# Windowed and global attention with a fused MLP: query columns in token order, with the global queries' inner scores apart

## The chip, the cores and the metric

The kernel runs on one core of one Trainium2 chip. The metric is the device time of one execution in microseconds (us). "Before" is the kernel as it stood, "after" is the same kernel with the change below.

## What is computed

Attention with 8 batches and 8 heads of width 64. Each head has 512 local tokens and 32 global tokens. Global queries see all 544 keys. Local queries see the 32 global keys and the local keys at most 32 positions away. The 4352 output tokens (544 a batch, global ones first), with the heads put side by side to 512 columns, then go through a two-layer network with a sigmoid-weighted activation. Cut to what matters:

```
k_all = concat([k_g, k_l]);  v_all = concat([v_g, v_l])       # per batch and head
out_g = softmax(scale * q_g @ k_all.T) @ v_all                # 32 x 64
s_ll  = where(|i - j| <= 32, scale * q_l @ k_l.T, -1e9)       # 512 x 512
s_lg  = scale * q_l @ k_g.T                                   # 512 x 32
out_l = softmax(concat([s_lg, s_ll])) @ concat([v_g, v_l])    # 512 x 64
x = concat([out_g, out_l]) as [8 * 544, 512]
h = x @ w_in                                                  # 512 -> 2048
out = (h * sigmoid(1.702 * h)) @ w_out                        # 2048 -> 512
```

Inputs and output are float32. The matmuls take bfloat16 operands and accumulate in float32.

## The kernel before

The order of all work is written out by hand (`manual_schedule`), and each engine runs its instructions in that order. A batch's eight heads are two **quads** of four heads (class `Quad`, with head `j` on the 32 partitions `32j` to `32j+31`; two of the 64 head columns lie in one 4-byte element). For each quad:

- `T` is `Tk` and `Tq`: VectorE transposes 32x32 blocks of the loaded keys and queries (tiles `rk`, `rq`) into `kT` and the query tile `qt` (four of them, used in turn). A loaded row holds 16 tokens, so a transposed block holds, for one `t` of 0 to 15, the tokens `16r+t` of all `r` of 0 to 31. `Tk` writes with a step, so that `kT` is in token order (L271). `Tq` writes its blocks one after the other, so that `qt` is ordered by `t`, then `r` (L275).
- `qt` has 24 such rows `t`: 16 of local queries and 4 at each end that `ext` (L285) fills with copies of the 32 global queries, cut into rows as wide as a window. A window is a range of `r` for each chunk `c` of 128 keys: `WIN = ((0, 10), (6, 12), (14, 12), (22, 10))`, that is 160 or 192 queries.
- `S(rnd)` (L314) computes the scores of two key chunks, `c = 2*rnd` and `2*rnd+1`, for the four heads. For each chunk and each half `e` of the head columns it issues four matmuls, one per head, each on its own 32 rows of the array and into its own PSUM bank. The moving operand is `q[p, lo:hi, r0:r0+nr, e]`: 20 or 19 rows `t` of 10 or 12 queries, 200 or 228 columns. Global and local queries of a chunk thus go in one matmul.
- `gk` (L333) multiplies global keys with queries: `K` for the local queries (512 columns, tile `kb`), `gg` for the global ones (32 columns).
- `X` exponentiates the scores on ScalarE into the tile `E` (L347), `XK` does it for `kb` (L383, with a DMA that copies the result to other partitions), `M` multiplies by the window mask on VectorE (L354), `eg` picks the blocks for the global queries.
- `U(unit)` (L426) adds up the softmax sums (unit 0) and the two halves of the output (units 1, 2) from `E` and `v`, four heads side by side on 32 array columns each; `ekU` (L400) adds the global keys' part. `Gm` (L444) does the global queries' output, four heads with 66 columns.
- `R` and `XL` divide by the sums into `xL`, `G` does so for the global queries into `xG`.

Then the network: `h_mm` (L495) makes 128 of the 2048 columns at a time for a batch's 512 local tokens, `h_act` (ScalarE tanh, VectorE multiply) makes `gT`, and `o_mm` (L520) makes tiles of 128 tokens by 512. `o_out` scales a tile on ScalarE into `ob` and sends it out (L542). Since the tokens of `xL` and `gT` are ordered by `t`, then `r`, a tile of 128 tokens is four groups of 32 rows that lie 16 rows apart in the output, and goes out by four DMAs from the SP queue. The global tokens of all batches are a ninth, narrower batch at the end.

`phase_o(i)` interleaves the output matmuls of batch `i` with the attention of batch `i+1`, two rounds `S` and one `UG` (`ekU`, `U`, `Gm`) per quad; the 16 `h_step` of a batch follow. The first two batches have an order of their own: quad 0 is loaded and transposed in halves, its first round is issued in two parts (`part=0` and `1`, after the first and the second half of `Tq`), and quads 0 and 1 add the mask to the scores by matmuls with an identity (`B`, L297) instead of `M`. Quad 2's `T`, `ext` and first `S` come after the `h_step` of batch 0. The transposition `Tq` of quad 4 and that of its global keys (`transpose_g`, tile `kgT`, L205) stand in the middle of quad 2's output work.

Of the kernel before, what the change touches and what calls it, by code (L numbers as in the profile page):

```python
# [20 lines left out]
def kernel(  # L21
# [24 lines left out]
    HD = D // 2  # L46
# [4 lines left out]
    RW = 428  # L51
# [118 lines left out]
    for i in range(4):  # L170
        qt = consts.tile([128, 24, 32], F32, name="q%d" % i)
        nc.vector.memset(qt[:, 0:4, :], 0.0)
        nc.vector.memset(qt[:, 20:24, :], 0.0)
        qtiles.append(qt)

    WIN = ((0, 10), (6, 12), (14, 12), (22, 10))
# [5 lines left out]
    bias = consts.tile([128, 16, 12], BF16)  # L182
    bandt = band.rearrange("p (r t) -> p t r", t=16)
    nc.vector.tensor_sub(ident, step[:, 65:193], step[:, 64:192])
    nc.vector.tensor_sub(band, step[:, 65:257], step[:, 0:192])
    nc.vector.tensor_scalar(bias, bandt, -1.0, 262144.0, op0=ALU.add, op1=ALU.mult)

    def near(t, c):
        lo = 0 if c else 2
        return t[:, :, lo : lo + WIN[c][1]]  # L190

    def make_mask(c):
        nr = WIN[c][1]
        at = (0, 160, 0, 192)[c]
        nc.scalar.activation(mask[:, c // 2, at : at + 16 * nr].rearrange("p (t r) -> p t r", t=16),
                             near(bandt, c), AF.Copy)

    qgT = consts.tile([128, NQ, 40], F32)
    nc.vector.memset(qgT[:, :, 32:], 0.0)
    kgT = consts.tile([128, NQ, 32], F32)  # L200
    def transpose_g(lo, hi, names="qk"):
        for name, dst, s in (("q", qgT, rqg), ("k", kgT, rkg)):
            if name not in names:
                continue
            nc.vector.transpose(dst[:, lo:hi, :32], s[:, lo:hi].bitcast(F32))  # L205
# [43 lines left out]
    class Quad:  # L249
        def __init__(self, Q):  # L250
            self.Q = Q
            self.b, self.u = divmod(Q, 2)
            if self.u == 0:
                xL[self.b] = att.tile([128, NKC, Sl], BF16, name="xL", bufs=2)
            self.x = xL[self.b]
            self.v = vtiles[self.b % 2][:, self.u]
            self.qt = qtiles[Q % 4]
            self.q = self.qt.bitcast(BF16).rearrange("p t (r e) -> p t r e", e=2)
            self.qg = qgT[:, Q, :32].bitcast(BF16).rearrange("p (s e) -> p s e", e=2)
            self.kg = kgT[:, Q].bitcast(BF16).rearrange("p (s e) -> p s e", e=2)  # L260
            self.E = [None, None]
            self.bk = {}
            self.st = {}
            self.pt = None
            self.gr = 1
# [8 lines left out]
        def Tq(self, lo=0, hi=16):  # L274
            nc.vector.transpose(self.qt[:, 4 + lo : 4 + hi, :].rearrange("p t r -> p (t r)"),  # L275
                                loaded[self.b][1][:, self.u].bitcast(F32)[:, 32 * lo : 32 * hi])
# [5 lines left out]
        def ext(self, cs=(0, 1, 2, 3)):  # L282
            for c in cs:
                (r0, nr), t0, n = WIN[c], (0, 20, 1, 20)[c], (4, 3, 3, 4)[c]
                nc.vector.tensor_copy(  # L285
                    self.qt[:, t0 : t0 + n, r0 : r0 + nr],
                    qgT[:, self.Q, : n * nr].rearrange("p (t r) -> p t r", t=n))


        def B(self, rnd, split=False, js=range(4)):  # L290
            if 0 in js:
                self.bk[rnd] = [pbank("s") for _ in range(4)] if split else self.spt(rnd)
            ps = self.bk[rnd] if split else [bank(self.bk[rnd], j) for j in range(4)]
            for c in (2 * rnd, 2 * rnd + 1):
                w = (40, 200, 36, 228)[c]
                for j in js:
                    nc.tensor.matmul(ps[j][:, w : w + 16 * WIN[c][1]], lhsT=ident, rhs=near(bias, c),  # L297
                                     start=(c == 2 * rnd), stop=False, skip_group_check=True)

        def S(self, rnd, split=False, added=False, part=None):  # L300
            if not added:
                self.bk[rnd] = self.spt(rnd)
            ps = self.bk[rnd] if split else [bank(self.bk[rnd], j) for j in range(4)]
            for c in (2 * rnd, 2 * rnd + 1):
                off = (0, 200, 0, 228)[c]
                r0, nr = WIN[c]
                t0, t1 = ((0, 20), (4, 23), (1, 20), (4, 24))[c]
                lo, hi = ((t0, t1) if part is None else (12, t1) if part else (t0, 12))
                off += (lo - t0) * nr
                n = (hi - lo) * nr  # L310
                for e in range(2):
                    for j in range(4):
                        p = slice(32 * j, 32 * j + 32)
                        nc.tensor.matmul(  # L314
                            ps[j][:, off : off + n],
                            lhsT=self.k[p, 128 * c : 128 * c + 128, e],
                            rhs=self.q[p, lo:hi, r0 : r0 + nr, e],
                            start=(e == 0 and not added), stop=(e == 1), skip_group_check=True,
                        )
            if not part:  # L320
                self.E[rnd] = att.tile([128, 4, RW + 32], BF16, name="e%d" % rnd)
            if split:
                self.gk(ps[2][:, RW : RW + 32], self.qg)
            self.ps = self.bk[rnd]


        def gk(self, out_, rhs, e=None):
            for ee in (0, 1) if e is None else (e,):
                for j in range(4):
# [4 lines left out]
                                     rhs=rv[:, :, ee] if len(rv.shape) == 3 else rv[:, :, :, ee],  # L334
# [16 lines left out]
        def M(self, rnd):  # L351
            at = 36 if rnd else 40
            e = self.E[rnd][:, :, at : at + LW]
            nc.vector.tensor_mul(e, e, mask[:, rnd : rnd + 1, :].to_broadcast([128, 4, LW]))  # L354

        def K(self, e=None):
            if e != 1:
                self.kb = pbank("kb")
            self.gk(self.kb, self.q[:, 4:20], e)
# [57 lines left out]
        def U(self, unit):  # L417
            ov = self.st[unit]
            h = unit - 1
            for c in range(4):  # L420
                r0, nr = WIN[c]
                at = (40, 200, 36, 228)[c]
                for j in range(4):
# [3 lines left out]
                        ov[32 * j : 32 * j + 32, :].rearrange("p (t r) -> p t r", t=16)[:, :, r0 : r0 + nr],  # L427
                        lhsT=lv, rhs=self.E[c // 2][:, j, at : at + 16 * nr],
# [3 lines left out]
        def Gm(self, og=None):  # L432
            if og is None:
                og = pbank("og")
            for c in range(5):
                for j in range(4):
                    if c < 4:
                        at = (0, 392, 0, 388)[c]
                        lv = self.E[c // 2][:, j, at : at + 32]
# [85 lines left out]
    def o_out(i, tci, op):  # L525
        ob = moe.tile([128, d_model], F32, name="ob", bufs=6)
        last = i == B and tci == B // 4 - 1
        for lo, hi in ((0, 320), (320, 512)) if last else ((0, 512),):
# [5 lines left out]
            nc.scalar.activation(ob[:, lo:hi], op[:, lo:hi], AF.Copy, scale=0.5)  # L534
            for j in range(4):
                eng = nc.scalar if last and j % 2 else nc.sync
                if i < B:
                    rows = out[i * S + Sg : (i + 1) * S, :].rearrange("(r t) m -> t r m", t=16)[4 * tci + j]
                else:
                    r = (4 * tci + j) * S  # L540
                    rows = out[r : r + Sg, :]
                eng.dma_start(out=rows[:, lo:hi], in_=ob[32 * j : 32 * j + 32, lo:hi])  # L542
# [22 lines left out]
    a.ext((0, 1))  # L565
# [5 lines left out]
    a.ext((2, 3))  # L571
# [257 lines left out]
```

## Time and profile before

| what | value |
|---|---|
| time, median of 3 runs | 307.43 us (307.39 to 307.59) |
| profiled execution, first to last instruction | 305.3 us, its own time is not given apart from this span |
| PE, DVE, ACT, POOL busy | 298.7, 211.2, 169.3, 55.7 us |
| granted PE clock | 1.00 throughout |
| score matmuls (L314) | 528, 21.2 us busy |
| DMA issues of output tiles from SP | 136, most of 64 KB, median 1.7 us to landing |

PE is the matmul side of TensorE and PEld its weight loads, DVE is VectorE, ACT is ScalarE, POOL is GpSimd, SP the queue that issues DMAs. Busy time is the union of an engine's instructions, so matmuls that overlap count once. A shape such as `32*128 32x228` is a tile of 32 array rows by 128 columns, with 228 moving columns.

### The profile page before, as it was taken

The page shows a single profiled execution, that of the slowest core. Times are in us where ns is not written, and L with a number is a line of the kernel's source. Part 1 is how long each engine was busy: PE and PEld are TensorE (multiplying, and loading weights), DVE is VectorE, ACT ScalarE, POOL GpSimd, SP SyncE. Part 2 cuts the span into 40 slices and gives each one's busy share as a digit, 9 for nine tenths or more (in the row PEclk, how much of TensorE's full clock was granted, in tenths as well). Part 3 has the DMA queues.
Part 4 walks back from the last instruction along what each step waited for, and adds up shares of the span by engine and source line. Part 5 has one row for each costly group of instructions (what it writes and reads, how often), then busy time and mean ns, then how long its engine had stood idle before and what let it go on. Part 6 is the DMA issues. An engine that isn't in the chain of part 4 may idle for free.

```text
span 305.3 us, 7862 instructions
## 1 busy us (share of the span) xinstructions
PE 298.7 (98%) x3265; PEld 148.5 (49%) x3265; DVE 211.2 (69%) x445; ACT 169.3 (55%) x282; POOL 55.7 (18%) x89
## 2 busy tenths in 40 slices
PE   7999999999999999999999999999999999999995
PEld 6454445445454455445454455445454454446653
DVE  6678858978868876777767876787677855573320
ACT  4738484585556655575457654665456661673421
POOL 8732755530050002300050002100000000000000
PEclk9999999999999999999999999999999999999999
DMA  7999999999399023941299024901130021101122
GB/s 191 178 206 207 197 180 230 211 170 131 82 112 191 10 56 84 151 97 37 54 122 170 4 56 89 101 0 48 44 86 2 2 66 48 46 0 36 36 63 75
DMA packets 56436, 29.52 MB, mean 97 GB/s; under 512 B 43088, under 2 KB 46288, under 8 KB 56400
## 3 DMA queue, kind: packets, MB, share of 16 engines
q0 software_dynamic: 46000, 16.98, 49.9%
q1 hardware_dynamic: 9920, 11.39, 14.3%
q10 hardware_dynamic: 480, 0.66, 0.7%
q8 instruction: 25, 0.41, 0.6%
q14 instruction: 11, 0.09, 0.1%
HBM read 35.13 MB, written 8.91 MB: 144 GB/s over the span
## 4 chain that ended last, share of the span: by engine, by line
PE 80%; DMA 15%; DVE 2%; POOL 1%; issue 1%; ACT 0%; ACTq 0%; DVEq 0%; POOLq 0%
PE op L520 34%; PE hp L495 33%; DMA rk<-in_k_l_dram 10%; PE s L314 5%; PE ov L426 4%; DMA rq<-in_q_l_dram 3%; DMA w_in_sb<-in_moe_w_in_dram 2%; PE ov L400 2%; DVE xL L459 1%; PE op L532 1%; PE s L444 1%; PE s L333 1%; ACTq L542 0%; ACT ob L534 0%; DVE e L354 0%
## 5 line engine op out<-in xcount | busy, mean ns | idle before, releaser
L520 PE MATMUL op<-w_out_sb,gT 128*128 128x512 bf16 x528 | 122.0, 380 | 0.0
L503 DVE SCALAR_TENSOR_TENSOR gT<-th,hp 128x512 bf16<-128x512 f32 (+1 forms) x140 | 91.2, 657 | 41.8 <-ACT th L502 40.7
L495 PE MATMUL hp<-xL,w_in_sb 128*128 128x512 bf16 x496 | 108.9, 379 | 0.3 <-DVE xL L459 0.2
L502 ACT ACTIVATE th<-hp 128x512 f32<-128x512 f32 (+1 forms) x140 | 79.9, 573 | 43.4 <-PE hp L495 39.9
L495 PEld LDWEIGHTS <-w_in_sb 128*128 128x128 bf16 x576 | 56.2, 98 | 64.7 <-issue 0.9
L520 PEld LDWEIGHTS <-gT 128*128 128x128 bf16 x528 | 49.2, 98 | 56.2 <-issue 3.5
L347 ACT ACTIVATE e<-s 128x856 bf16<-128x856 f32 x62 | 51.6, 884 | 12.1 <-PE s L444 7.0
L534 ACT ACTIVATE ob<-op 128x512 f32<-128x512 f32 (+2 forms) x35 | 20.5, 585 | 59.0 <-PE op L520 56.5
L89 POOL DMA_DIRECT2D v<-in_v_l_dram x24 | 18.7, 782 | 111.2 <-PE s L444 105.8
L450 DVE STREAM_TRANSPOSE sT<-ov 128x512 f32<-128x512 f32 x15 | 10.8, 717 | 26.9 <-PE ov L426 26.9
L354 DVE TENSOR_TENSOR e<-e,mask 128x1408 bf16<-128x1408 bf16 x28 | 24.4, 872 | 5.7 <-ACT e L347 5.7
L314 PE MATMUL s<-q,kT 32*128 32x228 bf16 (+5 forms) x528 | 21.2, 280 | 1.0 <-DVE q L275 1.0
L459 DVE TENSOR_TENSOR xL<-ov,rs 128x512 bf16<-128x512 f32 x30 | 19.3, 686 | 1.4
L314 PEld LDWEIGHTS <-kT 32*128 32x128 bf16 x528 | 10.9, 95 | 14.8 <-issue 6.6
L271 DVE STREAM_TRANSPOSE kT<-rk 128x512 f32<-128x512 f32 (+1 forms) x17 | 16.9, 994 | 1.0 <-DMA rk<-in_k_l_dram 1.0
L383 ACT ACTIVATE ek<-kb 128x512 bf16<-128x512 f32 x16 | 9.7, 608 | 9.2 <-PE kb L333 7.0
L426 PE MATMUL ov<-e,v 128*32 128x160 bf16 (+1 forms) x480 | 12.2, 239 | 0.0
L454 DVE STREAM_TRANSPOSE rs<-rT 128x512 f32<-128x512 f32 x16 | 11.4, 711 | 0.6
L275 DVE STREAM_TRANSPOSE q<-rq 128x512 f32<-128x512 f32 (+1 forms) x17 | 10.9, 641 | 1.0 <-ACT rq L558 1.0
L426 PEld LDWEIGHTS <-v 128*32 128x32 bf16 x512 | 10.0, 97 | 0.9 <-issue 0.9
L333 PE MATMUL kb<-q,kgT 32*32 32x512 bf16 x128 | 10.4, 387 | 0.0
L495 PE MATMUL hp<-xG,w_in_sb 128*128 128x256 bf16 x64 | 9.6, 273 | 0.0
(82 smaller groups left out, 170.6 us busy)
## 6 DMA issues: line engine op xcount, KB each, us to landing
out_dram<-ob SPq DMA_DIRECT2D x132, 64.0 KB, 1.7
v<-in_v_l_dram POOLq DMA_DIRECT2D x32, 128.0 KB, 6.0
rk<-in_k_l_dram POOLq DMA_DIRECT2D x6, 512.0 KB, 10.8
rq<-in_q_l_dram POOLq DMA_DIRECT2D x5, 512.0 KB, 8.6
w_out_sb<-in_moe_w_out_dram POOLq DMA_DIRECT2D x4, 512.0 KB, 10.8
rq<-in_q_l_dram POOLq DMA_DIRECT2D x5, 256.0 KB, 8.9
ek<-ek SPq DMA_DIRECT2D x13, 96.0 KB, 2.9
w_in_sb<-in_moe_w_in_dram POOLq DMA_DIRECT2D x4, 256.0 KB, 6.4
```

What stands on the lines that cost most here:

```text
L89: nc.gpsimd.dma_start(out=vtiles[b % 2][p, s, :, :, :D], in_=vf[b, g][:, hs])
L271: nc.vector.transpose(self.kT.rearrange("p (r t) -> p t r", t=16)[:, lo:hi], loaded[self.b][0][:, self.u].bitcast(F32)[:, 32 * lo : 32 * hi])
L314: nc.tensor.matmul(ps[j][:, off : off + n], lhsT=self.k[p, 128 * c : 128 * c + 128, e], rhs=self.q[p, lo:hi, r0 : r0 + nr, e], start=(e == ...
L347: nc.scalar.activation(e[:, 2 * i : 2 * i + 2, :RW], self.ps[i][:, :, :RW], AF.Exp, scale=scale)
L354: nc.vector.tensor_mul(e, e, mask[:, rnd : rnd + 1, :].to_broadcast([128, 4, LW]))
L426: nc.tensor.matmul(ov[32 * j : 32 * j + 32, :].rearrange("p (t r) -> p t r", t=16)[:, :, r0 : r0 + nr], lhsT=lv, rhs=self.E[c // 2][:, j, ...
L459: nc.vector.tensor_mul(self.x[:, 2 * self.u + h, :], self.st[1 + h], self.st["rs"])
L495: nc.tensor.matmul(hp[:, : width(i)], lhsT=w_in_c[:, fc // 8, kc, fc % 8 // 2, :, fc % 2], rhs=(xL[i] if i < B else xG)[:, kc, :], start=( ...
L502: nc.scalar.activation(th[:, :n], hp[:, :n], AF.Tanh, scale=0.851)
L503: nc.vector.scalar_tensor_tensor(gTs[i][:, fc, :n], in0=th[:, :n], scalar=1.0, in1=hp[:, :n], op0=ALU.add, op1=ALU.mult)
L520: nc.tensor.matmul(op, lhsT=gTs[i][:, fc, tci * 128 : tci * 128 + 128], rhs=w_out_sb[:, fc, :], start=(first and fc == 4 * f4), stop=(fc = ...
L534: nc.scalar.activation(ob[:, lo:hi], op[:, lo:hi], AF.Copy, scale=0.5)
```

## The change

The query tile holds the queries in token order: 32 global queries, the 512 local ones, and the 32 global ones again. `Tq` writes with a step as `Tk` does. `ext` becomes one copy that fills both ends. A window is a range of tokens, so that the columns of scores, of `E` and of the mask are contiguous token ranges, and PSUM columns of `U` too. For the outer chunks (0 and 3) the global queries adjoin the window, and one matmul of 192 columns covers both. For the inner chunks (1 and 2) they don't, so that there are two matmuls, of 192 and of 32 columns. Both use the same weights, which are loaded for each. In the split first round the local queries of each part are 8 of every 16 columns. `E` is 416 columns wide for a head instead of 428. Output tiles are 128 adjoining rows and go out by one DMA; those of the global tokens are unchanged. The memsets of the query tiles and of `qgT`'s padding go.

```diff
-    RW = 428
+    RW = 416
...
-        qt = consts.tile([128, 24, 32], F32, name="q%d" % i)
-        nc.vector.memset(qt[:, 0:4, :], 0.0)
-        nc.vector.memset(qt[:, 20:24, :], 0.0)
-        qtiles.append(qt)
-
-    WIN = ((0, 10), (6, 12), (14, 12), (22, 10))
+        qtiles.append(consts.tile([128, Sl + 2 * Sg], F32, name="q%d" % i))
+
+    WIN = ((0, 160), (96, 192), (224, 192), (352, 160))
+    AT = (32, 192, 32, 224)
+    GAT = (0, 384, 0, 384)
...
-    bias = consts.tile([128, 16, 12], BF16)
-    bandt = band.rearrange("p (r t) -> p t r", t=16)
+    bias = consts.tile([128, 192], BF16)
...
-    qgT = consts.tile([128, NQ, 40], F32)
-    nc.vector.memset(qgT[:, :, 32:], 0.0)
+    qgT = consts.tile([128, NQ, 32], F32)
...
         def Tq(self, lo=0, hi=16):
-            nc.vector.transpose(self.qt[:, 4 + lo : 4 + hi, :].rearrange("p t r -> p (t r)"),
+            nc.vector.transpose(self.qt[:, Sg : Sg + Sl].rearrange("p (r t) -> p t r", t=16)[:, lo:hi],
                                 loaded[self.b][1][:, self.u].bitcast(F32)[:, 32 * lo : 32 * hi])
...
-        def ext(self, cs=(0, 1, 2, 3)):
-            for c in cs:
-                (r0, nr), t0, n = WIN[c], (0, 20, 1, 20)[c], (4, 3, 3, 4)[c]
-                nc.vector.tensor_copy(
-                    self.qt[:, t0 : t0 + n, r0 : r0 + nr],
-                    qgT[:, self.Q, : n * nr].rearrange("p (t r) -> p t r", t=n))
+        def ext(self):
+            nc.vector.tensor_copy(
+                self.qt.rearrange("p (n w) -> p n w", w=Sg)[:, ::17],
+                qgT[:, self.Q : self.Q + 1].to_broadcast([128, 2, Sg]))
...
         def S(self, rnd, split=False, added=False, part=None):
...
-                off = (0, 200, 0, 228)[c]
-                r0, nr = WIN[c]
-                t0, t1 = ((0, 20), (4, 23), (1, 20), (4, 24))[c]
-                lo, hi = ((t0, t1) if part is None else (12, t1) if part else (t0, 12))
-                off += (lo - t0) * nr
-                n = (hi - lo) * nr
+                q0, w = WIN[c]
+                at = AT[c]
+                if part is None:
+                    runs = {0: ((0, 0, 192),), 1: ((at, Sg + q0, w), (GAT[c], 0, Sg)),
+                            2: ((at, Sg + q0, w), (GAT[c], 0, Sg)), 3: ((at, Sg + q0, 192),)}[c]
+                else:
+                    runs = ((at, Sg + q0, w),) if part else ((at, Sg + q0, w), (GAT[c], 0, Sg))
                 for e in range(2):
-                    for j in range(4):
-                        p = slice(32 * j, 32 * j + 32)
-                        nc.tensor.matmul(
-                            ps[j][:, off : off + n],
-                            lhsT=self.k[p, 128 * c : 128 * c + 128, e],
-                            rhs=self.q[p, lo:hi, r0 : r0 + nr, e],
-                            start=(e == 0 and not added), stop=(e == 1), skip_group_check=True,
-                        )
+                    for k, (o0, i0, n) in enumerate(runs):
+                        for j in range(4):
+                            p = slice(32 * j, 32 * j + 32)
+                            o, r = ps[j][:, o0 : o0 + n], self.q[p, i0 : i0 + n, e]
+                            if part is not None and k == 0:
+                                h = slice(8 * part, 8 * part + 8)
+                                o = o.rearrange("p (r t) -> p r t", t=16)[:, :, h]
+                                r = r.rearrange("p (r t) -> p r t", t=16)[:, :, h]
+                            nc.tensor.matmul(
+                                o, lhsT=self.k[p, 128 * c : 128 * c + 128, e], rhs=r,
+                                start=(e == 0 and k == 0 and not added), stop=(e == 1), skip_group_check=True,
+                            )
...
         def M(self, rnd):
-            at = 36 if rnd else 40
-            e = self.E[rnd][:, :, at : at + LW]
+            e = self.E[rnd][:, :, Sg : Sg + LW]
...
         def U(self, unit):
...
                     nc.tensor.matmul(
-                        ov[32 * j : 32 * j + 32, :].rearrange("p (t r) -> p t r", t=16)[:, :, r0 : r0 + nr],
-                        lhsT=lv, rhs=self.E[c // 2][:, j, at : at + 16 * nr],
+                        ov[32 * j : 32 * j + 32, q0 : q0 + w], lhsT=lv, rhs=self.E[c // 2][:, j, at : at + w],
...
     def o_out(i, tci, op):
...
+            if i < B:
+                r = i * S + Sg + 128 * tci
+                nc.sync.dma_start(out=out[r : r + 128, :], in_=ob)
+                continue
             for j in range(4):
                 eng = nc.scalar if last and j % 2 else nc.sync
-                if i < B:
-                    rows = out[i * S + Sg : (i + 1) * S, :].rearrange("(r t) m -> t r m", t=16)[4 * tci + j]
-                else:
-                    r = (4 * tci + j) * S
-                    rows = out[r : r + Sg, :]
-                eng.dma_start(out=rows[:, lo:hi], in_=ob[32 * j : 32 * j + 32, lo:hi])
+                r = (4 * tci + j) * S
+                eng.dma_start(out=out[r : r + Sg, lo:hi], in_=ob[32 * j : 32 * j + 32, lo:hi])
...
-    a.ext((0, 1))
+    a.ext()
...
     a.Tq(8, 16)
-    a.ext((2, 3))
```

More of the change, by code (lines that the diff above doesn't have):

```diff
@@ L45 @@
     NQ = B * 2
-    HD = D // 2
     NKC = d_model // 128
@@ L181 @@
     band = consts.tile([128, 192], BF16)
-    bias = consts.tile([128, 16, 12], BF16)
-    bandt = band.rearrange("p (r t) -> p t r", t=16)
+    bias = consts.tile([128, 192], BF16)
     nc.vector.tensor_sub(ident, step[:, 65:193], step[:, 64:192])
     nc.vector.tensor_sub(band, step[:, 65:257], step[:, 0:192])
-    nc.vector.tensor_scalar(bias, bandt, -1.0, 262144.0, op0=ALU.add, op1=ALU.mult)
+    nc.vector.tensor_scalar(bias, band, -1.0, 262144.0, op0=ALU.add, op1=ALU.mult)
     def near(t, c):
-        lo = 0 if c else 2
-        return t[:, :, lo : lo + WIN[c][1]]
+        lo = 0 if c else 32
+        return t[:, lo : lo + WIN[c][1]]
     def make_mask(c):
[L193 to L196, printed above, removed]
-    qgT = consts.tile([128, NQ, 40], F32)
-    nc.vector.memset(qgT[:, :, 32:], 0.0)
+        at = AT[c] - 32
+        nc.scalar.activation(mask[:, c // 2, at : at + WIN[c][1]], near(band, c), AF.Copy)
+    qgT = consts.tile([128, NQ, 32], F32)
     kgT = consts.tile([128, NQ, 32], F32)
@@ L204, in transpose_g @@
                 continue
-            nc.vector.transpose(dst[:, lo:hi, :32], s[:, lo:hi].bitcast(F32))
+            nc.vector.transpose(dst[:, lo:hi, :], s[:, lo:hi].bitcast(F32))
     def load_v2(b):
@@ L257, in __init__ @@
             self.qt = qtiles[Q % 4]
-            self.q = self.qt.bitcast(BF16).rearrange("p t (r e) -> p t r e", e=2)
-            self.qg = qgT[:, Q, :32].bitcast(BF16).rearrange("p (s e) -> p s e", e=2)
+            self.q = self.qt.bitcast(BF16).rearrange("p (m e) -> p m e", e=2)
+            self.qg = qgT[:, Q].bitcast(BF16).rearrange("p (s e) -> p s e", e=2)
             self.kg = kgT[:, Q].bitcast(BF16).rearrange("p (s e) -> p s e", e=2)
@@ L294, in B @@
             for c in (2 * rnd, 2 * rnd + 1):
-                w = (40, 200, 36, 228)[c]
+                w = AT[c]
                 for j in js:
-                    nc.tensor.matmul(ps[j][:, w : w + 16 * WIN[c][1]], lhsT=ident, rhs=near(bias, c),
+                    nc.tensor.matmul(ps[j][:, w : w + WIN[c][1]], lhsT=ident, rhs=near(bias, c),
                                      start=(c == 2 * rnd), stop=False, skip_group_check=True)
@@ L333, in gk @@
                     nc.tensor.matmul(out_[r : r + 32], lhsT=self.kg[p, :, ee],
-                                     rhs=rv[:, :, ee] if len(rv.shape) == 3 else rv[:, :, :, ee],
+                                     rhs=rv[:, :, ee],
                                      start=(ee == 0), stop=(ee == 1), skip_group_check=True)
@@ L358, in K @@
                 self.kb = pbank("kb")
-            self.gk(self.kb, self.q[:, 4:20], e)
+            self.gk(self.kb, self.q[:, Sg : Sg + Sl], e)
         def eg(self):
@@ L420, in U @@
             for c in range(4):
-                r0, nr = WIN[c]
-                at = (40, 200, 36, 228)[c]
+                q0, w = WIN[c]
+                at = AT[c]
                 for j in range(4):
@@ L437, in Gm @@
                     if c < 4:
-                        at = (0, 392, 0, 388)[c]
-                        lv = self.E[c // 2][:, j, at : at + 32]
+                        lv = self.E[c // 2][:, j, GAT[c] : GAT[c] + Sg]
                         rv = self.v[:, j, c, :]
```

## The prediction

> **What bounds the kernel now.** I read the page's busy shares first, then the table of stages, then the chain of waits in one steady stretch, and last the start times of single matmuls.
>
> ```profile
> span 305.3 us, 7862 instructions
> ...
> PE 298.7 (98%) x3265; PEld 148.5 (49%) x3265; DVE 211.2 (69%) x445; ACT 169.3 (55%) x282; POOL 55.7 (18%) x89
> ...
> PEclk9999999999999999999999999999999999999999
> ```
>
> PE is busy for 98% of the span at a full granted clock. No other engine passes 69%. A share that high can hide pipelined waiting, so I look at stages:
>
> ```profile
> 57.00:103.44 46.44, 46.33 (x465) 21.77 (x467) 36.94 (x78) 29.03 (x48) 9.80 (x13) 1.00 1.12 134
> 103.44:137.50 34.06, 34.06 (x389) 16.33 (x392) 25.51 (x53) 19.94 (x32) 4.51 (x6) 1.00 0.58 87
> 137.50:171.56 34.06, 34.06 (x389) 16.33 (x392) 25.50 (x53) 19.95 (x32) 4.50 (x6) 1.00 0.58 86
> ```
>
> The columns are the stage, its length, then PE, PEld, DVE, ACT and POOL busy. One batch takes 34.06 us, again and again, and PE fills it. The chain of waits inside one batch names only PE lines:
>
> ```profile
> 137.50 0.60 PE s L314 x16
> 138.10 3.56 PE op L520 x16
> 141.66 0.59 PE s L314 x16
> ...
> 142.88 1.03 PE ov L426 x47
> ```
>
> So from about 57 us on a nanosecond saved on PE is a nanosecond off the end, and DVE, ACT, SP and the transfers have room. Before that, three places hang on DVE (below).
>
> A **round** is one call of `S`: a quad (four heads) against two key chunks, 16 matmuls in the chain above. They run as four sets of four, one matmul per row group of 32 rows, started within about 10 ns of each other. From the start times of single matmuls in the timeline, a set of 200 columns is followed 114.9 ns later by the next (24 cases), one of 228 columns 133.8 ns later (30 cases). The `U` sets (L426) take 70.9 ns for 160 columns and 84.4 for 192, which is (84.4-70.9)/32 = 0.42 ns a column. The score sets lie well above: with the smaller sets of the first round (120 columns 70.8, 96 columns 59.0) the slope is (114.9-70.8)/80 = 0.55 ns a column in runs of 10 and (133.8-59.0)/132 = 0.57 in runs of 12. From the last 228-column set to the next line's first matmul it is 228.7, so leaving this mode adds 95 ns. A whole round, from its first start to the next line's first, is 114.9+113.4+2x133.8+95 = 591 ns.
>
> **Part 1, the scores.** After the change a round has four sets of 192 unbroken columns and two new sets of 32 (264 more matmuls in the program). 28 of the 32 rounds (quads 2 to 15, from 37 us on) stand on the PE path; the first four belong to the start, costed below. Two things are unknown: a 192-column set and a 32-column set.
>
> *The 192-column set.* If the excess over 0.42 ns a column is the price of reading `q` in runs of 10 or 12, the set falls to what a `U` set of 192 takes (84.4, or 81.9 before another shape; I take 83). If it comes from four row groups each writing 128 output rows, it stays: 114.9x192/200 = 110.3. No row shows this set, but one comes near:
>
> ```profile
> 10.97 0.63 PE L333 MATMUL kb<-q,kgT 32*32 32x512 bf16 x8
> ```
>
> These eight are two sets of four row groups, reading the same `q` tile with the same step of two elements, but 512 unbroken columns. The second set starts 239 ns after the first here, 225.5 in the other clean case: 0.44 to 0.47 ns a column, start-up included. So neither the step nor four row groups reading at once costs 0.55. What `kb` lacks is the short runs, and also the 128 output rows. A second sign is the slope, which differs with the run (0.55 and 0.57): an output limit would not know the run. Against it, the `bias` matmuls (L297) read runs of 10 and go at 70 ns for 160 columns like `U`, but with unit step. I take 83, with 110 as the other end.
>
> The score sets show 0.55 ns a column where `U`, whose output lies in PSUM in runs of 10 and 12, shows 0.42. [...]
>
> *The 32-column set.* Its weights are the ones just used, but they are loaded again. Nearest rows: four matmuls of 66 columns (L444) 33.2 ns, four of 32 columns at the head of `gg` (L333) 39.7, the smallest score set (80 columns) 40.5. Below, streaming alone is 32x0.42 = 13. I take 33, the row with as many weights (128x32) behind a short stream, with 13 and 41 as ends. [...]
>
> A round is then 4x83+2x33+95 = 493 ns, 98 less than 591. 28 x 98 = **2.74 us off** (ends: 28 x 138 = 3.9 and 28 x 82 = 2.3).
>
> **Part 2, DVE.** `Tq` now writes with a step, as `Tk` does: 1045 ns in place of 670, and the next DVE instruction starts 0.89 instead of 0.60 us later, +0.30 a quad. Against that three of four `ext` copies (181 ns each) go, and nine memsets at 1.5 to 3.3 us, where DVE then waits for transfers (0.57 us before L120). In steady state `T` and `ext` together get no longer (2.3 us), and the copies end at 140.69 for scores that start at 141.59, so 0.9 us of cover hides them. Three early places have no cover:
>
> ```profile
> 36.62 0.72 DVE L285 COPY q<-qgT 128x40 f32<-128x40 f32 x4
> 37.00 0.66 PE L314 MATMUL s<-q,kT 32*128 32x200 bf16 x16
> ...
> 49.35 0.67 DVE L275 STREAM_TRANSPOSE q<-rq 128x512 f32<-128x512 f32 x1
> 49.95 0.20 DVE L205 STREAM_TRANSPOSE kgT<-rkg 128x64 f32<-128x64 f32 x1
> 50.20 0.41 PE L333 MATMUL kb<-q,kgT 32*32 32x512 bf16 x4
> ```
>
> - At 37.00 the scores of quad 2 need the first two copies, done at 36.88. `Tq` moves them 0.30 later, one copy replaces two: 37.10, so PE stalls about 0.14.
> - At 50.20 `kb` needs `kgT`, done at 50.15. `Tq` stands ahead of it on DVE: +0.29, and everything of that quad queued behind it on PE waits too. The stalls at 54 and 56 us hang on the same DVE chain and move along unchanged.
> - At 8.25 the second half of the first round waits for the second half `Tq` (0.45, then some 0.62): +0.17. The round's remaining sets get shorter (2x96 for 2x132 columns, about -0.04) and six exps on ACT, which works without a gap from 8.7 to 14.7 us, lose 0.01 to 0.02 each: +0.05 left.
>
> Together **+0.48 us** (0.2 to 0.65, the low end if the first two are partly covered).
>
> **Part 3, what lies beside.** The exps read 832 columns instead of 856. Between 512 and 1024 columns ACT's tanh rows differ by 0.82 ns a column, so each is 20 ns shorter, 62 of them 1.2 us; ACT at 55% is not on the path: nothing. The mask multiply keeps its 1408 elements. The 32 tiles of 128 token rows leave by one 256 KB transfer each instead of four of 64 KB. SP loses 96 issues of 0.42 us, but SP spent 145 us waiting for `ob`, and the `ek` transfers queued behind them move the same bytes: nothing, and if a bigger transfer lands later, six `ob` buffers cover some 20 us. The last tile's own transfers are not changed. `U` and `Gm` keep columns and rate.
>
> **Sum.** Span 305.34 - 2.74 + 0.48 = 303.1. The runs' median, 307.43, lies 2.09 above the span (start and end outside the first and last instruction, untouched): **305.2 us**.
>
> **Rivals.**
> *A, the rate belongs to four row groups with 128 output rows.* A round is 4x110.3+2x33+95 = 602, so +11 ns x 28 = +0.3, with the DVE stalls +0.8: **308.2, slower** (307.1 with sets of 13 ns, 308.7 with 41). For it: no row with this tile shape has a slope near 0.42. Against it: the slope that follows the run length, and `kb`. It decides as soon as the 192-column set stays above about 104 ns.
> *B, the weight reload of the small sets is not hidden.* A score weight load is recorded at 95 ns, and 32 columns last 13. If a small set costs 65, a round is 557, -34 x 28 = -0.95, with the stalls **306.9**; at the full 95 it would be 308.6. The break-even is 73 ns. Against it: 80-column sets follow each other after 40.5 ns with the same loads.
>
> **Chances.** Forecast 0.60, A 0.25, B 0.15. What a measurement can tell from no change is about 0.2%, 0.6 us: 306.8 to 308.0. The forecast case is faster nearly throughout; A is slower for 0.19 and within for 0.06; B is split, 0.04 faster, 0.07 within, 0.04 slower. Rounded: faster 0.63, same 0.14, slower 0.23. The forecast's own range is 303.7 (small sets free, 0.2 of stalls) to 305.8; for eight in ten it has to reach into A: 304.0 to 308.6.
>
> **What would show it.** Right: the chain's score pieces fall from 0.60 to about 0.50 us for 24 matmuls, a batch from 34.06 to about 33.67, and new short PE waits on DVE appear near 37 and 50 us. Wrong: 192-column sets spaced by 104 ns or more (A), spacing after 32-column sets above 60 ns (B), a batch at 34.06 or more, or PE waits on DVE in steady state.

## The result and the profile after

After takes 311.07 us (median of five runs, 309.50 to 311.39), before 307.43 on the same chip (median of five, 307.04 to 308.08): a ratio of 1.011 [1.008, 1.013], so slower by about 1.1%, clear of the noise. (Ratios here compare undisturbed runs alone, so they can differ from those of the medians.) The profiled execution of after is the 309.50 one, with a span of 307.8 us, 2.5 more than before.

The busy line of the page, and then the table of stages (length, PE, PEld, DVE, ACT, POOL busy, granted clock, DMA share, GB/s), with the same steady stages that the prediction showed of before:

```profile
span 307.8 us, 8218 instructions
...
PE 296.5 (96%) x3529; PEld 150.0 (49%) x3529; DVE 209.4 (68%) x388; ACT 166.6 (54%) x282; POOL 55.8 (18%) x89
```

```profile
61.61:107.71 46.10, 45.98 (x504) 21.91 (x507) 36.54 (x68) 28.76 (x48) 7.89 (x11) 1.00 0.92 120
107.71:141.38 33.67, 33.67 (x420) 16.49 (x424) 25.48 (x47) 19.62 (x32) 4.52 (x6) 1.00 0.55 88
141.38:175.06 33.68, 33.68 (x421) 16.48 (x424) 25.50 (x47) 19.64 (x32) 4.52 (x6) 1.00 0.55 88
```

A steady batch takes 33.67 us in place of 34.06: the gain is there, and PE is busy 2.2 us less in all. The chain of waits in that batch (start, length, what) has the shorter score pieces:

```profile
107.71 0.51 PE s L313 x23
108.21 3.56 PE op L514 x16
```

The loss lies before the steady stages. Where the same piece of work starts in the two kernels shows in which stretch it arose:

| start of | before, us | after, us | after is late by |
|---|---|---|---|
| quad 0's last two `U` units | 15.25 | 15.74 | 0.49 |
| network of batch 0 | 18.38 | 21.69 | 3.31 |
| scores of quad 2 | 37.00 | 40.45 | 3.45 |
| network of batch 1 | 53.90 | 58.74 | 4.84 |
| network of batch 2 | 89.47 | 93.73 | 4.26 |
| end | 305.34 | 307.8 | 2.46 |

Two stretches lose most, the one from 15 to 22 us (2.82) and the one from 40 to 59 us (1.39, net of shorter scores). In each the chain of waits of after has a piece in which PE stops and that is no work of any engine:

```profile
18.14 0.33 PE ov L396 x4
18.46 0.34 PE ov L422 x9
18.80 2.62 issue
21.43 0.33 PE ov L422 x4
...
54.22 0.34 PE s L422 x9
54.55 1.42 issue
55.97 0.92 PE s L422 x34
```

"issue" means that the engine waited for nothing that the profile shows. PE stops in the middle of a `U` unit, all of whose inputs are there, and goes on with the next set of the same unit. The view of waits says the same of the weight loads (engine, line, releaser: us in all, times, longest), first before, then after:

```profile
PEld L426 <- issue: 6.4, 20, 0.4
```

```profile
PEld L422 <- issue: 10.0, 22, 2.9
PE ov L422 <- issue: 2.6, 1, 2.6
PE s L422 <- issue: 1.4, 1, 1.4
```

What is late is the instructions themselves. The page's DMA queues have a row that I passed over in before (queue, kind: packets, MB, share of 16 engines); here it is before and then after:

```profile
q8 instruction: 25, 0.41, 0.6%
```

```profile
q8 instruction: 27, 0.44, 0.6%
```

0.41 MB in 25 packets is 16 KB each. Counted in PE's order, a weight load and a matmul each as one, the first late instructions are the 702nd and the 1469th. With PE's own few semaphore instructions, which the trace lists as well, they are the 706th and the 1474th, 768 apart. The packets ahead of the two stops start at 18.95 and 53.68 us, and between them come those at 25.02 and 44.40: from the one to the other three packets for 768 instructions, 256 each. In every trace below with one of the two stops the first late instruction is again the 706th or the 1474th. So PE's program arrives in pieces of 256. The change adds 264 matmuls with as many weight loads: 80 of these 528 instructions come before 18 us, 144 before 50 us, and two pieces more.

With piece ends every 256 from the 191st instruction on (weight loads and matmuls alone counted, which puts the two ends at about 703 and 1471), the early part of the trace lines up in one way: when PE crosses into a piece, the piece after the next end is asked for, its packet moves some time later, and where PE stops, the instructions behind that end run 1.3 to 1.7 us after the packet has landed. That the crossing is what asks for the packet is my reading of these times. For the two stops, and for the same pieces in before:

| kernel, next end | crossed, us | packet, us | next piece runs |
|---|---|---|---|
| before, 703 | 15.51 | 18.98 to 19.92 | 22.06, no stop |
| after, 703 | 15.08 | 18.95 to 19.84 | 21.43, stop of 2.9 |
| before, 1471 | 48.00 | 51.17 to 52.14 | 55.36, no stop |
| after, 1471 | 49.45 | 53.68 to 54.67 | 55.97, stop of 1.7 |

(Stops are counted here from the last start to the next; the chain leaves out the work still running, so it has 2.62 and 1.42.) In after it is 6.3 and 6.5 us from crossing to running. Before had 6.6 and 7.4 us of work between its piece ends; after has the ends shifted into stretches with many small matmuls, where PE goes through 256 instructions in 3.4 and 4.9 us. In the steady batches of after, packets start between 2.5 us before and 1.4 us after PE's own crossing, so what asks for them can run somewhat ahead of PE, and no such stop occurs.

### The profile page after: what moved, and what is told of

Its sections match the earlier page's. It is cut to its first block, busy times and chain, and to the rows that moved or that the text cites. A ratio compares the mean times of both kernels' runs of the same rounds, so it can differ in the third digit from the quotient of the medians.

```text
span 307.8 us, 8218 instructions
## 1 busy us (share of the span) xinstructions
PE 296.5 (96%) x3529; PEld 150.0 (49%) x3529; DVE 209.4 (68%) x388; ACT 166.6 (54%) x282; POOL 55.8 (18%) x89
## 4 chain that ended last, share of the span: by engine, by line
PE 88%; DVE 4%; ACT 3%; DMA 2%; issue 2%; SPq 0%; ACTq 0%
PE hp L489 36%; PE op L514 35%; PE ov L422 5%; PE s L313 5%; PE ov L396 3%; DMA q<-in_q_l_dram 2%; PE s L489 1%; DVE gT L497 1%; DVE q L269 1%; ACT th L496 1%; PE op L526 1%; PE s L330 1%; DVE kT L265 1%; PE s L438 1%; PE kb L330 1%
## 5 line engine op out<-in xcount | busy, mean ns | idle before, releaser
L344 ACT ACTIVATE e<-s 128x832 bf16<-128x832 f32 x62 | 50.4, 864 | 12.2 <-PE s L438 7.0
L313 PE MATMUL s<-q,kT 32*128 32x192 bf16 (+3 forms) x792 | 18.4, 219 | 1.4 <-DVE rkg L119 1.2
L313 PEld LDWEIGHTS <-kT 32*128 32x128 bf16 x792 | 12.3, 92 | 14.4 <-issue 7.6
L269 DVE STREAM_TRANSPOSE q<-rq 128x512 f32<-128x512 f32 (+1 forms) x17 | 16.4, 965 | 1.0 <-ACT rq L552 1.0
```

The costliest lines, as they stand in the source:

```text
L269: nc.vector.transpose(self.qt[:, Sg : Sg + Sl].rearrange("p (r t) -> p t r", t=16)[:, lo:hi], loaded[self.b][1][:, self.u].bitcast(F32)[:, ...
L313: nc.tensor.matmul(o, lhsT=self.k[p, 128 * c : 128 * c + 128, e], rhs=r, start=(e == 0 and k == 0 and not added), stop=(e == 1), skip_grou ...
L344: nc.scalar.activation(e[:, 2 * i : 2 * i + 2, :RW], self.ps[i][:, :, :RW], AF.Exp, scale=scale)
```

## The experiments

Theory F is this: PE ran out of instructions. R1: the stops belong to what the changed kernel does at those places. R2: the 256 KB output transfers hold up a queue. Where a number below stands against "before", that kernel ran on the same chip, 307.1 to 307.7 us in the median.

**More instructions in the kernel before.** Nothing of the change, only more and smaller warm-up matmuls (with their weight loads 82 instructions more, for 3588 columns in place of 3584):

```diff
-    keep(28, psP.tile([128, 512], F32, name="w", tag="p"), 128)
+    keep(69, psP.tile([128, 512], F32, name="w", tag="p"), 52)
```

> The kernel before, with 82 more instructions in PE's stream and no other edit: the 28 warm-up matmuls of 128 columns become 69 of 52 columns (about the same 3 us). Theory F (PE ran out of instructions): the stream is brought by transfers of 16 KB, 256 instructions each, and a piece that is used up before the next one is there stalls PE. Then the kernel before gets the two stalls too, at about 18 and 52 us, marked as idle with no releaser, of 1 to 2.5 us each: 308.5 to 312 us. Rival R1 (the stalls belong to what the changed kernel does there, its unbroken scores, PSUM columns or waits): no stall, 307.4 +- 0.4 us. Rival R2 (the 256 KB output transfers block a queue): no stall, 307.4.

310.48 us against 307.42: the kernel before becomes slower by 1.0058 [1.0017, 1.0099] through 82 instructions that add next to no columns. The profiled execution had a mean granted clock of 0.56 (505.6 us), and its stops can't be read from it. The same kernel once more:

> The kernel before with 82 PE instructions more in its warm-up (69 matmuls of 52 columns for 28 of 128), a second time, for its profile. F: two waits of PE that nothing in the profile explains, about 2.2 us near 18 us and 1.9 us near 54 us, at program positions 703 and 1471, in a kernel that has neither the new scores nor the big output transfers. R1 and R2 (big output transfers in the queues): none.

309.53 us, and the timeline of PE (start, busy, line, operation, names, shapes, count, idle time before with its releaser) has both stops, in the lines of `U`:

```profile
17.41 0.34 PE L426 MATMUL ov<-e,v 128*32 128x160 bf16 x8
19.22 0.34 PE L426 MATMUL ov<-e,v 128*32 128x192 bf16 x8 [1.48 <-issue]
...
52.23 0.62 PE L426 MATMUL s<-e,v 128*32 128x160 bf16 x23
54.55 0.39 PE L426 MATMUL s<-e,v 128*32 128x192 bf16 x9 [1.70 <-issue]
```

The first late instructions are the 706th and the 1474th again, and the stops are 1.7 and 2.0 us from weight load to weight load. This kernel has neither the new scores nor the large transfers: R1 and R2 fall as causes of the stops.

**Fewer instructions in the changed kernel.**

```diff
-    keep(28, psP.tile([128, 512], F32, name="w", tag="p"), 128)
+    keep(7, psP.tile([128, 512], F32, name="w", tag="p"), 512)
```

> The changed kernel with 42 fewer PE instructions: 7 warm-up matmuls of 512 columns in place of 28 of 128, the same 3 us. F: the boundary between two pieces moves by 42 instructions, from inside U to the long MLP matmuls behind it, where an instruction pair lasts 0.22 us instead of 0.02; the first stall shrinks from 2.9 to about 0.5 to 1.5 us, the second (1.6 us) stays or shrinks a little: 308 to 310 us. R1 and R2: 311 us, both stalls unchanged.

306.71 us, 0.9937 [0.9903, 0.9971] of before. Seven wider warm-up matmuls turn a slower kernel into a faster one. That is better than the 308 to 310 expected: with the long stop the slow clock of most runs went too (below), ten of these eleven having a mean clock of 0.997 or more. The stops were 0.9 and 2.1 us in the profiled run, which at 310.64 us was the longest of the eleven and waited 3.6 us for two of DVE's transpositions ahead of 12 us (after 1.2).

In the next one the mask matmuls of `B` are merged too, one of 352 columns per bank in place of two:

```diff
-            for c in (2 * rnd, 2 * rnd + 1):
-                w = AT[c]
-                for j in js:
-                    nc.tensor.matmul(ps[j][:, w : w + WIN[c][1]], lhsT=ident, rhs=near(bias, c),
-                                     start=(c == 2 * rnd), stop=False, skip_group_check=True)
+            for j in js:
+                nc.tensor.matmul(ps[j][:, Sg : Sg + LW], lhsT=ident, rhs=bias[:, 160 * rnd : 160 * rnd + LW],
+                                 start=True, stop=False, skip_group_check=True)
```

> As e2, and the two bias matmuls of a bank in one of 352 columns: 74 fewer PE instructions than the changed kernel ahead of 18 us. F: no first stall, as in the kernel before, the second 0 to 1.6 us; with nothing else changed the forecast's sum returns: 305.2 without, 306.8 with the second stall. R1 and R2: 311 us.

306.47 us, 0.9962 [0.9928, 0.9997]. The first stop is gone, the second is 1.0 us from weight load to weight load.

**Is it the other warm-up?** The same seven matmuls in the kernel before:

> The kernel before, its warm-up of 28 matmuls of 128 columns done as 7 of 512 (the same columns, 42 PE instructions fewer, weight loads included). Theory F (PE's instructions arrive in pieces of 256, some 6.4 us after the piece before was entered while loads run): the piece ends move 42 instructions later in the work, and with 6.4 us laid over the start times of the kernel before this gives stalls of about 1.5 us near 16 us and 1.1 us near 50 us, where the kernel before has 0.1 in all: slower by about 2 us, 309 to 310, although it issues less. Theory R1 (the stalls belong to what the changed kernel does at those places): no stall, 307.0 to 307.6. That the other warm-up by itself is what helped the two runs with fewer instructions: faster by about 1 us.

307.96 against 307.66, 1.0003 [0.9975, 1.003]. The warm-up by itself brings nothing, as F wants. But F's own stops did not come either. The trace says why: the ends were crossed at 11.50 and 16.63, and at 43.98 and 49.23, only 5.1 and 5.3 us apart, but the packets between had started 2.8 us after the crossing, not 3.2 to 4.2 as in the table, and that was soon enough. The delay is not one number of 6.4 us. It depends on what else is being moved, which the next runs test.

**Does the packet wait behind loads?** A first try moved `load_v(2)` and `load(3)` down in the program, to just ahead of `load_v(3)`:

> The changed kernel with the loads of v for batch 2 and of q and k for batch 3 issued some 10 us later, behind the attention of batch 1, so that they don't run while the piece due at 54 us is on its way. If pieces are late because they queue behind data transfers: the first stall stays (2.9 us), the second (1.6 us) is gone or under 0.5: about 309.5 us. If a piece takes 6 us regardless: both stay, 311 us. R1 and R2: both stay, 311 us.

311.15 us, both stops there (2.95 and 1.1 us). It was no test: nothing else stands between the two places in POOL's queue, and POOL issued `load(3)` at 50.4 and 51.1 us instead of 49.8 and 50.5. Behind `load_v(3)`, which waits for PE, the loads are really late:

```diff
-    load_v(2)
-    load(3)
...
     load_v(3)
+    load_v(2)
+    load(3)
```

> The changed kernel with load_v(2) and load(3) put behind load_v(3), which waits for PE until 57 us, so that some 1.5 MB of transfers leave the stretch from 46 to 57 us. PE's own instructions are the same. Theory F with the piece waiting behind these transfers: the piece asked for near 49.5 us starts within about 1 us instead of 4.2, the stall near 54 us (1.4 us) is gone, the one near 18 us (2.8 us) stays; about 309.6. F with a fixed delay, or a theory in which the stall belongs to PE's work there: the second stall stays, 311.

The share of the DMA engines from the crossing to the packet is seen in the view of the DMA queues (queue: packets, MB, share). After, from 49.4 to 53.7 us:

```profile
q0 software_dynamic: 1459, 0.41, 99.7%
q1 hardware_dynamic: 288, 0.52, 36.1%
```

and with the loads moved, from 51.5 to 54.0 us, the packet (q8) included:

```profile
q1 hardware_dynamic: 332, 0.58, 61.7%
q8 instruction: 1, 0.02, 3.6%
q0 software_dynamic: 3, 0.00, 0.9%
```

The shares of after add up to 136%, so the recorded times of its packets overlap, which I read as packets that wait in line; with the loads moved it is 66%. With POOL's queue (q0) empty the packet starts 0.8 us after the crossing (51.67 to 52.44) instead of 4.2, and the second stop is gone; the large output transfer on q1 does not hold it. The first stop, under the loads of the weights, stays at 2.95 us. The time, 310.23 us, falls by 0.8, less than the 1.4 expected. These are four runs (309.31 to 310.77), and the profiled one lost 0.5 us more than that of after at the start, where PE waits for the queries (1.7 us in place of 1.2).

**The clock after the stop.** What the first stop costs beyond itself is in the stages of this run and of the one before (columns as above; the third from the end is the granted clock). First with the loads behind `load_v(3)`:

```profile
20.00:22.00 2.00, 0.03 (x4) 0.03 (x6) 0.97 (x3) 0.00 (x0) 0.72 (x1) 1.00 1.12 209
22.00:24.00 2.00, 2.00 (x12) 0.78 (x12) 1.29 (x4) 0.00 (x0) 0.35 (x1) 0.62 1.12 210
24.00:26.00 2.00, 2.00 (x6) 0.73 (x5) 0.00 (x0) 0.00 (x0) 0.30 (x1) 0.53 1.13 214
26.00:28.00 2.00, 2.00 (x30) 0.83 (x28) 0.12 (x1) 0.85 (x1) 0.54 (x1) 1.00 1.11 207
```

and in the other:

```profile
22.00:24.00 2.00, 2.00 (x12) 0.73 (x6) 1.29 (x4) 0.00 (x0) 0.17 (x2) 0.50 1.12 211
24.00:26.00 2.00, 2.00 (x7) 0.67 (x5) 0.00 (x0) 0.00 (x0) 0.51 (x1) 0.50 1.13 215
26.00:28.00 2.00, 2.00 (x7) 0.76 (x6) 0.00 (x0) 0.00 (x0) 0.54 (x1) 0.58 1.13 210
```

After PE's idle time of nearly 3 us the clock is halved, from 22.48 to 25.89 us in the first of these runs and from 20.84 to 27.67 in the other. Matmuls of 512 columns then follow each other after 426 ns in place of 216. That loses some 1.7 and 3.0 us on top of the stop, an estimate: half of the time in which PE worked there. It doesn't happen each time. The profiled run of after has full clock (mean 0.999) and 309.5 us; its other four runs have a mean of 0.993 to 0.994 and 310.8 to 311.4 us. Of the 19 runs of the three kernels with a stop of 2.9 us, 15 have a mean clock below 0.995, those at or above it take 308.6 to 309.5. Of 30 runs of three kernels without such a stop (the kernel before with 42 instructions fewer, and the last version below with its counterpart of before), 5 do, and of 89 runs of before itself, 15. So some 1.6 us of the loss in the median (311.07 against 309.50) goes with the clock.

The traces also suggest what decides it. In these two the changes of the clock lie 3.41 us apart or a multiple of it (6.83, 13.65, 17.07). Counted on in such steps, the same stop falls differently. In after, whose clock became full at 6.63 us, it lies across two of them (1.5 and 1.1 us without PE work), and the clock stays full:

```profile
16.87:20.28 3.41, 1.92 (x53) 0.95 (x49) 3.02 (x7) 0.52 (x1) 1.24 (x2) 1.00 1.19 202
20.28:23.70 3.42, 2.27 (x17) 1.07 (x17) 1.45 (x5) 0.00 (x0) 1.18 (x2) 1.00 1.10 205
```

With the loads behind `load_v(3)`, and then in the other run, one step has 2.6 and 1.8 us without PE work, and the clock halves at its end:

```profile
19.07:22.48 3.41, 0.79 (x18) 0.29 (x11) 1.97 (x6) 0.00 (x0) 1.34 (x2) 1.00 1.11 210
22.48:25.89 3.41, 3.41 (x10) 1.20 (x9) 1.16 (x4) 0.00 (x0) 0.65 (x1) 0.50 1.14 215
```

```profile
17.43:20.84 3.41, 1.65 (x49) 0.86 (x46) 2.89 (x6) 0.24 (x1) 1.24 (x2) 1.00 1.15 208
20.84:24.26 3.42, 2.55 (x13) 0.90 (x13) 1.29 (x4) 0.00 (x0) 1.11 (x2) 0.50 1.13 212
```

So in these traces whole steps of 3.41 us have a share of 1.00 or 0.50, and the steps with 2.6 and 1.8 us without PE work were followed by half the clock, those with 1.5 and 1.1 us by the full one. That the place of a stop in such steps decides is my reading; it fits that most but not all runs with the same 2.9 us of stop have a mean clock below 0.995 (15 of 19).

**A version with neither stop.** To the kernel with 74 instructions fewer come the moved loads, and quad 4's `Tq` and `kgT` transpose ahead of quad 2's `U` and `R`:

```diff
     c.X(1, lambda: c.XK(False))
+    nq[2][0].Tq()
+    transpose_g(4, 6, "k")
     for unit in range(3):
         a.U(unit)
     a.R()
-    nq[2][0].Tq()
-    transpose_g(4, 6, "k")
```

> The changed kernel with 74 PE instructions fewer (warm-up and bias matmuls as in the run with 74 fewer, 306.5), the two loads moved as above, and Tq and the kgT transpose of quad 4 issued on DVE ahead of R of quad 2. F: neither stall near 20 nor near 52 us (0.9 us less), and kb of quad 4 waits 0.3 us less for DVE: 305.2 to 305.6, below the kernel before by 2 us. If only the DVE order counts: 306.2. R1: no change from 306.5.

306.58 against 307.66, 0.9977 [0.9954, 0.9999]: hardly better than without (306.47). `kb` no longer waits, but the scores of quad 3 waited 0.5 us for a load that landed later (DVE began `Tk` at 41.93 instead of 41.16). And a stop of 1.3 us was left: PE is earlier here than with the moved loads alone (51.67): it crosses at 47.74 and finds the loads issued before 46 us still in the queue; the packet starts at 51.19. So more had to go:

```diff
-        nc.gpsimd.dma_start(out=loaded[2][0], in_=kf[2])
-        nc.gpsimd.dma_start(out=loaded[2][1][:, 1], in_=qf[2][:, 1])
+        nc.gpsimd.dma_start(out=loaded[2][0][:, 0], in_=kf[2][:, 0])
...
     load_v(3)
+    load(2, (1,))
     load_v(2)
     load(3)
```

> The run with 74 fewer, moved loads and the early Tq, in which the second half of batch 2's q and k (512 KB) is moved behind load_v(3) as well, so that less lies in the queue when the piece of instructions is asked for near 47.7 us. F with the piece waiting behind these transfers: it starts near 49 us (51.2 in the last run), and the 1.3 us stall near 52 us goes; 305.0 to 305.6 against 306.6 of the last run. F with a delay that does not depend on the queue: 306.6 again.

304.74 against 307.14, 0.9912 [0.9881, 0.9942]. The packet starts at 49.59, 1.0 us after the crossing at 48.58, the piece runs at 52.97, and `U`'s longest wait for instructions is that of before:

```profile
PEld L420 <- issue: 5.6, 21, 0.4
```

This version beats both kernels.

> The same kernel with each 128-token output tile leaving as four transfers of 64 KB again, as in the kernel before: one part of the change undone. The forecast (SP waits anyway, this part is worth nothing): the same time as the run beside it within 0.3 us. R2 (the 256 KB transfers delay what is queued with them): faster by over 0.5 us. If SP's 96 more issues of 0.42 us hold up the ek transfers: slower by some tenths.

305.09 us beside 304.74, 0.9937 [0.9908, 0.9967] of before. One transfer per tile or four makes no difference that these runs can tell: R2 fails here too, and the forecast's "nothing" stands.

Last, the same moves in the kernel before:

> The kernel before with the same moves of loads and of quad 4's Tq that brought the changed kernel to 304.7 us. F: the kernel before has no wait for instructions to lose (its piece asked for near 48 us came in time), so the moved loads bring nothing and the early Tq at most 0.2 us: 307.0 to 307.5, and the 2.4 us between the two kernels with the same care are the change's own. If the moved loads were what made that run fast in any kernel: 305 to 306.

307.19 against 307.49, 0.9998 [0.9952, 1.0043]. The moves bring it nothing, and the wider warm-up alone had brought it nothing either (1.0003). What the merged mask matmuls are worth in the kernel before was not run. But for these, the 2.4 us between the two kernels are the change's own, once its instructions come in time.

**What the short runs cost.** The forecast's gain rested on runs of 10 and 12 being slow, for which I had no reason. Ten blocks of 16 score-like sets behind the end of the kernel before (the expectation says nine) differ in the layout of the moving operand alone:

> The kernel before with nine blocks of 16 score-like sets (four 32x128 weight tiles, one per row group, 192 or 200 columns) added behind its end, which differ only in how the moving operand lies: unbroken, runs of 12 at element 6 and at element 8 of each row of 32, runs of 10 at 0 and at 22, runs of 8 at 0 and at 2, runs of 16 at 0, all with a step of 4 bytes, and runs of 12 at 6 and at 8 with a step of 2 bytes. If the price is that of any break, all but the first cost more than 90 ns a set. If it is that of a run which begins or ends inside a 16-byte line, runs of 12 at 8, of 8 at 0 and of 16 at 0 go at 80 to 85 and the others at 100 to 115. If the line is 32 bytes, runs of 12 at 8 are slow too and only 8 at 0 and 16 at 0 are free. If the price belongs to the four row groups, all are slow, the unbroken one too.

The timeline of PE:

```profile
301.97 1.56 PE L816 MATMUL s<-q,kT 32*128 32x192 bf16 x64
303.57 2.02 PE L819 MATMUL s<-q,kT 32*128 32x192 bf16 x64
305.61 1.68 PE L822 MATMUL s<-q,kT 32*128 32x192 bf16 x64
307.31 2.02 PE L825 MATMUL s<-q,kT 32*128 32x200 bf16 x64
309.35 2.02 PE L828 MATMUL s<-q,kT 32*128 32x200 bf16 x64
311.39 1.55 PE L831 MATMUL s<-q,kT 32*128 32x192 bf16 x64
312.95 2.34 PE L834 MATMUL s<-q,kT 32*128 32x192 bf16 x64
315.31 1.65 PE L837 MATMUL s<-q,kT 32*128 32x192 bf16 x64
316.97 2.03 PE L840 MATMUL s<-warm,kT 32*128 32x192 bf16 x64
319.01 1.54 PE L843 MATMUL s<-warm,kT 32*128 32x192 bf16 x64
```

From the starts of single matmuls, without each block's first set, and with the groups of four elements, counted from the row's start, that a set touches:

| line | runs | ns a set | groups of four | ns a group |
|---|---|---|---|---|
| L816 | unbroken 192 | 85.4 | 48 | 1.78 |
| L819 | 12 from element 6 | 112.9 | 64 | 1.76 |
| L822 | 12 from 8 | 91.5 | 48 | 1.91 |
| L825 | 10 from 0 | 113.4 | 60 | 1.89 |
| L828 | 10 from 22 | 113.1 | 60 | 1.89 |
| L831 | 8 from 0 | 83.4 | 48 | 1.74 |
| L834 | 8 from 2 | 133.6 | 72 | 1.86 |
| L837 | 16 from 0 | 90.1 | 48 | 1.88 |
| L840 | 12 from 6, step 2 bytes | 113.4 | 64 | 1.77 |
| L843 | 12 from 8, step 2 bytes | 82.4 | 48 | 1.72 |

In this probe the time follows the number of groups of four elements touched, at 1.7 to 1.9 ns each, whether the elements lie 4 or 2 bytes apart. Neither "any break" nor a line of 16 or 32 bytes fits: runs of 8 go at full rate from 0 and at the worst rate from 2, and runs of 12 from 8 with a step of 2 bytes, which end inside a 16-byte line, are free. A 228-column set of before, 19 runs of 12 from element 6, touches 76 groups: 76 x 1.76 = 134, and it took 133.8.

## Why the prediction was wrong

**The step that failed** is the account of the stretch before 57 us: "three places hang on DVE", and the sum built on it, 305.34 - 2.74 + 0.48. The 264 added matmuls were costed by what PE takes to run them. That they must also be delivered, and that the pieces after them end at other places, had no term. Measured: 2.8 us lost with the first stop and 1.4 us of waiting at the second in the profiled run, and some 1.6 us of halved clock in the median. Neither rival had it: rival A's range reached 308.7, and its mechanism is not what made the kernel slower.

A smaller term was off as well. The 2.09 us between span and median held a difference between runs: time less span is 1.7 to 1.8 us in every run that has both, so a span of 305.34 belongs to a run of some 307.0, not to the median.

**Scores: right.** The 192-column sets were followed after 84 to 101 ns (mean 89.1 ahead of a small set, 89.8 ahead of another large one; forecast 83), the 32-column sets after 26.0 (forecast 33, range 13 to 41). The two errors offset in part: a steady round takes 500 ns (forecast 493), against 593 in before (591), and a batch lost 0.39 us, forecast 4 x 0.098. Rival A needed 104 and rival B 65. The reason I gave for the slow rate, short runs, was close, but it is where they begin and end, not how long they are (in the probe runs of 8 took 83 or 134 ns). The 0.42 ns a column of `U` came from few sets: over the steady batches of before 160 columns take 73 ns and 192 take 82, which leaves the 83 as it was.

**DVE's early places: right where I looked.** PE's idle time ahead of quad 2's scores grew by 0.14 us (forecast 0.14), ahead of `kb` of quad 4 by 0.26 (0.29). At the second part of the first round it took 0.66 us from the start of the transposition to the scores, in before 0.50: 0.16 more (0.17). One place was missed: the scores of quad 5 in the first `phase_o`, at 77.9 us, wait 0.19 us more, since the 0.9 us of cover that I took from a later batch is not there yet.

**The start:** 0.49 us by the `U` sets of quad 0, where I had 0.05 left of the third place. The chain of waits of after runs there from the load of the queries' second half through ACT's cast and DVE's transposition to the scores. ACT's cast begins at 7.56 us, in before at 7.09: 0.47 of the 0.49 is the later landing; the longer transposition and the shorter pieces behind it nearly cancel. I can only put the landing down to chance, since in the traces of all versions of the two kernels this cast begins between 6.5 and 8.0 us. The first mask matmuls ran at the slow clock until 6.6 us instead of 5.8, but PE then waited 1.17 us for these scores (0.96 in before), so that cost nothing. **ACT, output transfers, SP:** nothing, as forecast.

The stretches sum up: 0.49 at the start, 2.82 with the first stop, 0.14 for quad 2, 1.39 to batch 1 (a stop of 1.4 to 1.7, 0.26 for `kb`, less the shorter scores), and then 2.38 given back by shorter rounds: 2.46 in all. The version that is fed in time took 304.74 us, near the forecast of 305.2. It carries the wider warm-up, the early `Tq` and the merged mask matmuls as well, so it is no clean measure of the forecast, and that the two lie so near is in part luck.

Could it have been seen? The margin could. The rows of instruction packets stood in the trace of before, and the packet at 51.17 to 52.14 us served work due at 55.36. That a shift of 80 instructions would use that margin up followed only from knowing where the pieces end, and the trace of before has no stop that shows it.

## What to carry to other kernels

Where a change adds many small instructions to an engine that is full, look at the queue of instruction packets in the trace: here, where PE worked through 256 instructions in 3.4 and 4.9 us while large loads were in flight, it ran dry, and the whole program behind shifted. Wide warm-up matmuls instead of narrow ones, and loads issued no earlier than needed, made room and cost nothing here (1.0003 and 0.9998 in the kernel before). Choose the layout of a moving operand that four row groups read, as in the probe, so that its runs begin and end at multiples of four elements (there runs of 8 took 83.4 ns a set from element 0, 133.6 from 2).

## What the chip showed that I had not expected

- PE's program comes in packets of 16 KB. From crossing into a piece to running the one behind it took 6.3 and 6.5 us at the stops of after (the packet started 3.9 and 4.2 us after the crossing). Where the load queue was empty it started after 0.8 to 1.1, and 4.4 to 5 us were enough.
- 82 instructions with next to no extra columns cost the kernel before 0.6% [0.2, 1.0].
- A stop of 2.9 us was followed by half the clock in most runs, for 3.4 and 6.8 us in the two traces that show it: in one of them that came after a step of 3.4 us with 1.8 us without PE work.
- In the probe four row groups read as if in groups of four elements: the same 192 columns take 83 or 134 ns, by whether runs of 8 begin at element 0 or 2.
